# A retention and feed-forward kernel in written order: each engine's sequence fixed by the code, a serial first block, weights converted later, and a new layout of q, k and v

## The chip, the cores and the metric

The kernel runs on one core of one Trainium2 chip. The metric is the device time of one execution in microseconds (us): the median of repeated runs. Times within one execution come from one profiled execution, counted from the start of its span.

## The reference

The kernel computes retention, that is attention with a fixed decay instead of a softmax, and a feed-forward layer on top of it. Batch is 8, heads 8, sequence 576, head size 64; the model width is 512 and the hidden width 2048.

```python
scores = scale * np.matmul(q, k.transpose(0, 1, 3, 2))
gamma = 1.0 - 2.0 ** (-5.0 - np.arange(H, dtype=np.float32))
Dmat = np.where(rel >= 0, gamma[:, None, None] ** rel[None, :, :], 0.0)
attn_out = np.matmul(scores * Dmat[None], v)
x = attn_out.transpose(0, 2, 1, 3).reshape(B * S, H * D)
h = x @ w_in
return (h - np.tanh(h)) @ w_out
```

The two weights are float64 arrays; q, k and v are float32.

## The kernel before

**Chunks.** The sequence is cut into nine chunks of 64 positions. A chunk of all eight batches is a block of 512 columns, and the blocks are numbered n = 0 to 8. Retention runs chunk by chunk with a running state in SBUF: for each batch, scores within the chunk, a mask, the product with v, plus the state times q. q and v are first multiplied by tables of decay powers (`qtab`, `vtab`) on GpSimd (POOL), lines 134 and 135, for the first chunk 328 and 329. Each product is many 64x64 matmuls issued by `run` (L171).

**Items of the feed-forward layer.** The hidden width is 16 tiles f of 128. `mm1(n, f)` is twelve 128x512 matmuls (L229): float32 precision comes from splitting x and the weight into a high and a low part and adding three products. `activate` computes g = h - tanh(h): tanh on ScalarE (ACT, L242), the subtraction on VectorE (DVE, L243), the rounding to the high part `gh` on ACT (L244) and the low part `gl` on DVE (L245). `mm2(n, f)` is twelve matmuls (L278) that add into the PSUM tile `o` of four groups t. At f = 15 the groups are finished one after the other: each group's three matmuls are followed by a copy `ob`, on ACT for t = 0 and 2 (L285), on DVE for t = 1 and 3 (L287), and by two stores.

**Entries.** `entry(p, sc)` is the retention of a pair of batches of the next chunk: 64 small matmuls (scores of pair p+1, outputs and states of pair p), the mask `pm` (L180), the new x in `xh` (ACT, L195) and `xl` (DVE, L196), the state's addition (L216), then the load of pair p+2 and its preparation on POOL. Four entries lie in a chunk.

**The first block.** Chunk 0 has no work to hide behind. Its eight batches j come one at a time, with the data in buffers that w_out takes over later. Scores run two batches ahead of the outputs. Before it, 14 matmuls on a zeroed tile `warm` (L298) keep TensorE (PE) at work. The PSUM tile `spare` holds scores, new state and most of the outputs.

**Weights.** They arrive as float64 and are turned into two float32r parts on the chip: two ACT operations make a guard mask (L62, L63), three DVE operations on integers assemble the bits (L71, L73, L75), ACT rounds the high part (L77) and DVE subtracts the low part (L78). This is called a conversion or a unit; there are 32, 16 for w_in and 16 for w_out. `steps(k)` advances it by a number of DVE operations, `ready(k)` completes k of them.

**The stages.** First the first block; then n = 0 and n = 1, in which only `mm1` runs and h is stored to DRAM (`spill`, copied by ACT at L234) because w_out isn't converted yet; then the 32 spilled items are fetched back (`fetch`), activated (`resume`, L260 to L263) and multiplied (`mm2`); and for n = 2 to 8 a loop of `mm1(n, f)`, an entry where f % 4 == 1, and `mm2` of the item before.

**What sets the order.** A scheduler orders each engine's instructions by estimated times and dependencies; so the order of an engine needn't be that of the code. A dependency is kept per tile: a matmul into one group of `o` waits for a copy that reads another group of it. All loads and stores are issued by SyncE's queue (SP).

## Time and profile before

| | us |
|---|---|
| median of 3 runs | 930.42 (930.21 to 931.33) |
| profiled execution | 931.84 |
| its span | 930.1 |
| PE busy | 895.2 (96%) |
| DVE busy | 367.1 (39%) |
| ACT busy | 282.7 (30%) |
| POOL busy | 97.2 (10%) |
| mean granted TensorE clock | 0.977 |

In the rows of a profile, PE is TensorE's matmuls and PEld its weight loads, which overlap them; L229 is line 229 of the kernel; x12 is a count of instructions. A row of the timeline has the start, the duration, the engine, the line and the operation with out<-in, and in brackets the idle time before it with what released it. A row of the waits has who waited for whom, the total, how often, and the longest. A row of the stages has, after each engine's busy time, the granted clock as a share of full speed, the DMA engines' share and what they moved.

### The profile page before, as it was taken

Reading aid. Unit: us, or ns where it says so; the run is one execution under the profiler, and the core shown is the slowest. Engines: PE = TensorE matmul, PEld = TensorE weight load, DVE = VectorE, ACT = ScalarE, POOL = GpSimd, SP = SyncE. Lnnn points to the kernel's source line nnn. Section 1 sums busy time; section 2 is a strip of 40 time slices with the busy share of each in tenths; the row PEclk is TensorE's granted clock in tenths of the full one; section 3 lists DMA queues with packets and bytes.
Section 4 is the critical chain, followed back from the end, with each engine's and each line's share of the span. In section 5 each row is a group of like instructions: output and inputs, shape, how many; then the busy total and the mean of one; then the engine's idle time right before and its main releaser. Section 6 shows DMA issues by size and latency. Waiting matters only on the chain.

```text
span 930.1 us, 17611 instructions
## 1 busy us (share of the span) xinstructions
PE 895.2 (96%) x7822; PEld 732.7 (79%) x7822; DVE 367.1 (39%) x543; ACT 282.7 (30%) x483; POOL 97.2 (10%) x84
## 2 busy tenths in 40 slices
PE   6698899999999999999999999999999999999997
PEld 4586688787878888888888888888888888888885
DVE  3989911654533333333332343333232332223222
ACT  2686522644422222222222222222222222222221
POOL 5204210000010000000100010001100100000000
PEclk7599899999999999999999999999999999999999
DMA  8787645434231113111311131112111221001001
GB/s 297 283 289 249 265 175 179 116 102 125 81 91 52 47 46 92 52 46 47 92 47 51 45 89 42 39 32 75 53 51 47 66 72 47 1 1 46 1 1 45
DMA packets 27004, 83.11 MB, mean 89 GB/s; under 512 B 3760, under 2 KB 4912, under 8 KB 22832
## 3 DMA queue, kind: packets, MB, share of 16 engines
q1 hardware_dynamic: 26928, 81.99, 27.2%
q8 instruction: 61, 1.00, 0.5%
q14 instruction: 15, 0.12, 0.1%
HBM read 64.15 MB, written 17.83 MB: 88 GB/s over the span
## 4 chain that ended last, share of the span: by engine, by line
PE 88%; DVE 6%; DMA 2%; issue 1%; ACT 1%; POOL 1%; SPq 0%; DVEq 0%; ACTq 0%
PE o L278 43%; PE h L229 38%; PE s L171 3%; PE own L171 2%; PE new L171 2%; DMA a<-in_qkv_dram 1%; DVE mi L71 1%; DVE mi L73 1%; DVE mo L71 1%; DVE wi L78 1%; DMA rwo<-in_w_out_dram 1%; DVE mo L73 1%; DVE mi L75 0%; DMA spill_dram<-g 0%; DVE wo L78 0%
## 5 line engine op out<-in xcount | busy, mean ns | idle before, releaser
L229 PE MATMUL h<-xh,wi 128*128 128x512 f32 x1152 | 309.5, 393 | 1.2 <-ACT xh L195 0.9
L278 PE MATMUL o<-wo,gh 128*128 128x512 f32 x1152 | 294.4, 394 | 4.4 <-ACT gh L262 1.7
L229 PEld LDWEIGHTS h<-xh,wi 128*128 128x128 f32 x1152 | 216.9, 189 | 47.2 <-ACT xh L195 1.1
L278 PEld LDWEIGHTS o<-wo,gh 128*128 128x128 f32 x1152 | 212.4, 188 | 52.9 <-ACT ob L285 3.9
L243 DVE TENSOR_TENSOR g<-h,g 128x512 f32<-128x512 f32 x112 | 77.4, 691 | 375.5 <-ACT g L242 375.5
L242 ACT ACTIVATE g<-h 128x512 f32<-128x512 f32 x112 | 67.0, 598 | 398.7 <-PE h L229 397.8
L278 PE MATMUL o<-wo,gl 128*128 128x512 f32 x576 | 158.5, 389 | 0.0
L229 PE MATMUL h<-xl,wi 128*128 128x512 f32 x576 | 155.1, 391 | 0.0
L229 PEld LDWEIGHTS h<-xl,wi 128*128 128x128 f32 x576 | 108.9, 189 | 23.1
L278 PEld LDWEIGHTS o<-wo,gl 128*128 128x128 f32 x576 | 108.1, 188 | 22.6
L134 POOL TENSOR_TENSOR a<-a,qtab 128x512 f32<-128x512 f32 x32 | 47.6, 1487 | 672.1 <-DMA a<-in_qkv_dram 660.6
L245 DVE TENSOR_TENSOR gl<-g,gh 128x512 fp32r<-128x512 f32 x112 | 84.1, 751 | 74.2 <-ACT gh L244 59.1
L244 ACT CAST gh<-g 128x512 fp32r<-128x512 f32 x112 | 69.5, 620 | 82.3 <-DVE g L243 79.1
L171 PE MATMUL own<-a,state 64*64 64x64 f32 x1024 | 65.4, 224 | 0.0
L171 PE MATMUL own<-pm,a 64*64 64x64 f32 x1024 | 63.7, 222 | 0.0
L171 PEld LDWEIGHTS own<-a,state 64*64 64x64 f32 x1024 | 53.1, 137 | 1.1 <-issue 1.1
L171 PEld LDWEIGHTS own<-pm,a 64*64 64x64 f32 x1024 | 53.1, 138 | 0.4 <-issue 0.4
L171 PEld LDWEIGHTS s<-a 64*64 64x64 f32 x1024 | 33.6, 137 | 22.1 <-issue 12.4
L171 PE MATMUL s<-a 64*64 64x64 f32 x1024 | 38.9, 225 | 8.4 <-POOL a L134 8.4
L135 POOL TENSOR_TENSOR a<-a,vtab 128x512 f32<-128x512 f32 x32 | 38.7, 1211 | 0.0
L216 DVE TENSOR_TENSOR state<-new,state 128x512 f32<-128x512 f32 x28 | 19.2, 686 | 38.8 <-PE own L171 38.8
L171 PE MATMUL new<-a 64*64 64x64 f32 x896 | 33.6, 225 | 0.0
(47 smaller groups left out, 459.3 us busy)
## 6 DMA issues: line engine op xcount, KB each, us to landing
a<-in_qkv_dram SPq DMA_DIRECT2D x32, 1024.0 KB, 5.5
out_dram<-ob SPq DMA_DIRECT2D x72, 128.0 KB, 2.4
rwi<-in_w_in_dram SPq DMA_DIRECT2D x16, 512.0 KB, 10.2
spill_dram<-g SPq DMA_DIRECT2D x32, 256.0 KB, 3.4
rwo<-in_w_out_dram SPq DMA_DIRECT2D x16, 512.0 KB, 5.3
s<-spill_dram SPq DMA_DIRECT2D x32, 256.0 KB, 2.6
a<-in_qkv_dram SPq DMA_DIRECT2D x8, 512.0 KB, 8.8
qtab<-in_qtab_dram SPq DMA_DIRECT2D x9, 128.0 KB, 2.1
```

Source lines behind the costliest of these rows:

```text
L71: nc.vector.scalar_tensor_tensor(z, hw, 3, z, op0=ALU.logical_shift_left, op1=ALU.bitwise_and)
L73: nc.vector.scalar_tensor_tensor(z, lw, 29, z, op0=ALU.logical_shift_right, op1=ALU.bitwise_or)
L134: nc.gpsimd.tensor_tensor(a[:, :, 0], a[:, :, 0], qtabs[c].unsqueeze(1).broadcast_to([P, 2, 4, C]), op=ALU.mult)
L135: nc.gpsimd.tensor_tensor(a[:, :, 2], a[:, :, 2], vtab[:, c].unsqueeze(1).unsqueeze(3).broadcast_to([P, 2, 4, D]), op=ALU.mult)
L171: nc.tensor.matmul(out_, w, x, start=start, stop=stop)
L216: nc.vector.tensor_tensor(st, new, st, op=ALU.add)
L229: nc.tensor.matmul(hp, win[f][:, a, cc, :], x[:, cc, :], start=(k == 0), stop=(k == 3 * NCC - 1))
L242: nc.scalar.activation(g, h, AF.Tanh)
L243: nc.vector.tensor_tensor(g, h, g, op=ALU.subtract)
L244: nc.scalar.copy(gh, g)
L245: nc.vector.tensor_tensor(gl, g, gh.bitcast(F32), op=ALU.subtract)
L278: nc.tensor.matmul(o[:, t], g[:, t * P : (t + 1) * P], wout[f][:, a, :], start=(f == 0 and k == 0), stop=(f == NF - 1 and k == 2),)
```

## The change

The change has five parts. A new function adds, at the end of the program, a dependency from each instruction to the one before it on its engine, so that every engine issues in the order in which the code is written. The first block is one batch at a time, with filler matmuls on `warm` after the scores and after the outputs, a PSUM tile of its own for the new state, and an early Tanh on ACT on which the warm-up's matmuls wait. The conversion is cut into units of three steps, with the low part's subtraction put into the next unit's first step; a step stands before and two behind each `mm1` of n = 0 and of three in four f of n = 1, and the rest goes with the resumed items. q, k and v are laid out in DRAM with each batch of a chunk contiguous (a pair's load then has two pieces of 4 KB for each partition instead of one of 8 KB). The first table `qtab0` gets a place in a buffer that w_out's eighth tile takes later, so that `qtab1` needn't wait for its last use.

```diff
+def in_order(tc):
+    before = {}
+    for ins in tc.nc.cur_bb.bb.instructions:
+        if ins.engine in before:
+            tc.add_manual_dep(
+                ins, before[ins.engine],
+                mybir.DependencyInfo(mybir.DependencyClass.NoSync, mybir.DependencyReason.DATA), reason="in_order",
+            )
+        before[ins.engine] = ins.name
...
+    def unit(k):
+        t, f = stream[k]
+        hw, lw = wraw[t, f][:, :, 1], wraw[t, f][:, :, 0]
+        z = masks.pop((t, f))
         nc.vector.scalar_tensor_tensor(z, hw, 3, z, op0=ALU.logical_shift_left, op1=ALU.bitwise_and)
+        finish()
         yield
+        if 0 < k and k + 1 < at_["load"]:
+            upto("guard", k + 2)
         nc.vector.scalar_tensor_tensor(z, lw, 29, z, op0=ALU.logical_shift_right, op1=ALU.bitwise_or)
         yield
         nc.vector.scalar_tensor_tensor(z, hw, -0x40000000, z, op0=ALU.bitwise_and, op1=ALU.bitwise_or)
...
         nc.scalar.copy(w[:, 0], z.bitcast(F32))
-        nc.vector.tensor_tensor(w[:, 1], z.bitcast(F32), w[:, 0].bitcast(F32), op=ALU.subtract)
...
+        last.append((w, z))
+    def finish():
+        while last:
+            w, z = last.pop()
+            nc.vector.tensor_tensor(w[:, 1], z.bitcast(F32), w[:, 0].bitcast(F32), op=ALU.subtract)
...
-            qtabs[c] = pool.tile([P, 4, C], F32, tag="qtab", bufs=1, name=f"qtab{c}")
+            if c == 0:
+                qtabs[c] = const.tile([P, 4, C], F32, tag="wo7", name="qtab0")
...
-        nc.sync.dma_start(a, qkv_d[c, :, 2 * pr : 2 * pr + 2])
+        nc.sync.dma_start(a, qkv_d[c, 2 * pr : 2 * pr + 2].rearrange("u p t i s -> p u t i s"))
...
     nc.vector.memset(warm, 0.0)
+    nc.scalar.activation(warm[:, :1], warm[:, :1], AF.Tanh)
...
+        sc, o = spare[:, j % 2, :4], spare[:, 2 + j % 2, :4]
+        new = psp.tile([P, 4, D], F32, tag="h", bufs=2, name=f"new_first{j}")
+        run(m_score(j, sc), [])
+        busy(1, 64)
+        after_score(j, sc.unsqueeze(1), 1)
+        if 4 <= j < 7:
+            step()
         run(m_state(j, new), m_out(j, o))
+        if j < B - 1:
+            busy(1, 64)
+        else:
+            busy(4)
         after_out(j, o.unsqueeze(1), 1)
         nc.scalar.copy(state[:, j], new)
...
+    units(2)
+    prep(B // 2)
     prep(B // 2 + 1)
...
-            upto("load", 9 + 3 * f // 4 if n == 0 else NF + 4 + f)
-            ready(f + 3 if n == 0 else NF + 3 * (f + 1) // 4)
+            upto("load", 10 + 3 * f // 4 if n == 0 else NF + 5 + f)
+            if n == 0 or f % 4 < 3:
+                step()
             mm1(n, f)
+            if n == 0 or f % 4 < 3:
+                step()
+                step()
...
-        if n == 0:
-            ready(NF + 12 + (f + 2) // 2)
+        for _ in range(2):
+            step()
         mm2(n, f)
...
     mm2(*prev)
+    in_order(tc)
```

The first place is PE in the first block, at batch 0. Before, with `a_86` and `a_90` the data of batches 0 and 1, and `pm_140` the masked scores of batch 0:

```order
L171 MATMUL spare<-a_86 64x64 [waits DMAHW1_49,Pool_49]
L171 MATMUL spare<-a_86 64x64 x7
L171 MATMUL spare<-a_90 64x64 [waits DMAHW4_49,DVE_49,Pool_49]
L171 MATMUL spare<-a_90 64x64 x7
L171 MATMUL spare<-a_86 64x64 [waits DVE_49]
```

And now, with `a_87` and `a_91` the same two batches, `pm_142` batch 0's masked scores and `new_first` its new state:

```order
L189 MATMUL spare<-a_87 64x64 [waits DMAHW1_49,Pool_49]
L189 MATMUL spare<-a_87 64x64 x7
L318 LDWEIGHTS warm
L318 MATMUL wps<-warm 64x512
L189 MATMUL new_first_132<-a_87 64x64 [waits Pool_49]
L189 MATMUL new_first_132<-a_87 64x64
L189 MATMUL spare<-pm_142,a_87 64x64 [waits DVE_49]
```

Batch 1's scores stood ahead of batch 0's state and outputs; now they stand behind them and a second filler, and wait for DVE there.

The second place is ACT at the end of chunk 2, where `g_0` and `gh_0` belong to item (3, 0), `ob_0` and `ob_2` to chunk 2's output. Before:

```order
L244 CAST gh_15_3362<-g_15_3361 128x512
L242 ACTIVATE g_0_3393<-h_0_3380 128x512
L285 COPY ob_0_3403<-o_2689 128x512
L244 CAST gh_0_3394<-g_0_3393 128x512
L285 COPY ob_2_3417<-o_2689 128x512
```

And now:

```order
L262 CAST gh_15_3389<-g_15_3388 128x512
L260 ACTIVATE g_0_3420<-h_0_3407 128x512
L262 CAST gh_0_3421<-g_0_3420 128x512
L303 COPY ob_0_3430<-o_2716 128x512
L303 COPY ob_2_3444<-o_2716 128x512
```

The first copy has moved behind item (3, 0)'s cast.

The third place is PE at the same chunk end, where `h_1` is item (3, 1) and `o` chunk 2's output. Before, from the first group on:

```order
L278 MATMUL o_2689<-wo_2006,gl_15_3363 128x512 [waits DVE_49]
L229 MATMUL h_1_3428<-xh_2680,wi_399 128x512 x4
L278 MATMUL o_2689<-wo_2006,gh_15_3362 128x512 [waits Activation_49]
L278 MATMUL o_2689<-wo_2006,gh_15_3362 128x512
L278 MATMUL o_2689<-wo_2006,gl_15_3363 128x512
L229 MATMUL h_1_3428<-xl_2681,wi_399 128x512 x4
```

And now:

```order
L296 MATMUL o_2716<-wo_1952,gl_15_3390 128x512 [waits DVE_49]
L296 MATMUL o_2716<-wo_1952,gh_15_3389 128x512 [waits Activation_49]
L296 MATMUL o_2716<-wo_1952,gh_15_3389 128x512
L296 MATMUL o_2716<-wo_1952,gl_15_3390 128x512
L296 MATMUL o_2716<-wo_1952,gh_15_3389 128x512 [waits DVE_49]
L296 MATMUL o_2716<-wo_1952,gh_15_3389 128x512
```

The matmuls of item (3, 1) stood between the groups; now they stand behind the last group. In the same way the matmuls of items (2, 0) and (2, 1), which stood between the last `mm1` of n = 1 and the first resumed `mm2`, now stand behind all 32 resumed items.

More of the change, by code (lines that the diff above doesn't have):

```diff
@@ L64, in guard @@
         masks[t, f] = m
-    def convert(t, f):
-        raw = wraw.pop((t, f))
-        hw, lw = raw[:, :, 1], raw[:, :, 0]
+    def unit(k):
+        t, f = stream[k]
+        hw, lw = wraw[t, f][:, :, 1], wraw[t, f][:, :, 0]
         z = masks.pop((t, f))
-        w = const.tile([P, 2, DM], F32R, tag=f"w{t}{f}", name=f"w{t}{f}")
         nc.vector.scalar_tensor_tensor(z, hw, 3, z, op0=ALU.logical_shift_left, op1=ALU.bitwise_and)
+        finish()
         yield
+        if 0 < k and k + 1 < at_["load"]:
+            upto("guard", k + 2)
         nc.vector.scalar_tensor_tensor(z, lw, 29, z, op0=ALU.logical_shift_right, op1=ALU.bitwise_or)
@@ L75, in convert @@
         nc.vector.scalar_tensor_tensor(z, hw, -0x40000000, z, op0=ALU.bitwise_and, op1=ALU.bitwise_or)
-        yield
+        del wraw[t, f]
+        w = const.tile([P, 2, DM], F32R, tag=f"w{t}{f}", name=f"w{t}{f}")
         nc.scalar.copy(w[:, 0], z.bitcast(F32))
-        nc.vector.tensor_tensor(w[:, 1], z.bitcast(F32), w[:, 0].bitcast(F32), op=ALU.subtract)
-        if t == "o":
-            wout[f] = w
-        else:
-            win[f] = w.rearrange("p s (c m) -> p s c m", m=P)
+        (wout if t == "o" else win)[f] = w if t == "o" else w.rearrange("p s (c m) -> p s c m", m=P)
+        last.append((w, z))
[3 more added lines that the diff above has]
+            nc.vector.tensor_tensor(w[:, 1], z.bitcast(F32), w[:, 0].bitcast(F32), op=ALU.subtract)
     stream = [(t, f) for t in "io" for f in range(NF)]
     at_ = {"load": 0, "guard": 0, "convert": 0}
-    going = []
+    last, going = [], []
     def upto(what, n):
@@ L91, in upto, with step, units @@
             at_[what] += 1
-    def steps(n):
-        for _ in range(n):
-            if not going:
-                if at_["convert"] == 2 * NF:
-                    return
-                upto("guard", at_["convert"] + 1)
-                going.append(convert(*stream[at_["convert"]]))
-                at_["convert"] += 1
-            if next(going[0], "end") == "end":
-                going.pop()
-    def ready(n):
+    def step():
+        if not going:
+            if at_["convert"] == 2 * NF:
+                return finish()
+            upto("guard", at_["convert"] + 1)
+            going.append(unit(at_["convert"]))
+            at_["convert"] += 1
+        if next(going[0], "end") == "end":
+            going.pop()
+    def units(n):
         while at_["convert"] < min(n, 2 * NF) or going:
-            if at_["convert"] < n:
-                upto("guard", at_["convert"] + 2)
-            steps(1)
+            step()
     loaded, scored, xs, qtabs = {}, {}, {}, {}
@@ L115, in load_qtab @@
         if c not in qtabs:
-            qtabs[c] = pool.tile([P, 4, C], F32, tag="qtab", bufs=1, name=f"qtab{c}")
+            if c == 0:
+                qtabs[c] = const.tile([P, 4, C], F32, tag="wo7", name="qtab0")
+            else:
+                qtabs[c] = pool.tile([P, 4, C], F32, tag="qtab", bufs=1, name=f"qtab{c}")
             nc.sync.dma_start(qtabs[c], qtab_d[c])
@@ L293, in retention_ffn, with busy @@
     nc.vector.memset(warm, 0.0)
+    nc.scalar.activation(warm[:, :1], warm[:, :1], AF.Tanh)
     wps = psp.tile([P, BLK], F32, tag="new", bufs=1, name="wps")
-    def busy(n):
+    def busy(n, rows=P):
         for _ in range(n):
-            nc.tensor.matmul(wps, warm[:, :P], warm, start=True, stop=True)
+            nc.tensor.matmul(wps[:rows], warm[:rows, :rows], warm[:rows], start=True, stop=True)
     busy(WARM)
-    load_qtab(0)
     def load_first(j):
         loaded[j] = const.tile([P, 4, 4, C], F32, tag=f"wo{NF - 1 - j}", name=f"a{j}")
-        nc.sync.dma_start(loaded[j], qkv_d[0, :, j])
+        nc.sync.dma_start(loaded[j], qkv_d[0, j])
+    load_qtab(0)
     load_first(0)
@@ L315, in retention_ffn @@
         load_first(j)
-    upto("load", 4)
+    upto("load", 5)
     load_pair(B // 2)
-    upto("load", 6)
+    upto("load", 7)
     load_pair(B // 2 + 1)
-    upto("load", 8)
+    upto("load", 9)
     spare = psp.tile([P, 4, 8, C], F32, tag="o", bufs=1, name="spare")
-    owns = [spare[:, 3, :4], spare[:, 3, 4:], psp.tile([P, 4, C], F32, tag="own", bufs=1, name="own_first")]
-    def first_prep(j):
+    for j in range(B):
         a = loaded[j]
@@ L329, in first_prep @@
         nc.gpsimd.tensor_tensor(a[:, 2], a[:, 2], vtab[:, 0].unsqueeze(2).broadcast_to([P, 4, D]), op=ALU.mult)
-    def first_score(j):
-        run(m_score(j, spare[:, j % 3, :4]), [])
-        after_score(j, spare[:, j % 3, :4].unsqueeze(1), 1)
-    first_prep(0)
-    first_prep(1)
-    first_score(0)
-    first_score(1)
-    for j in range(B):
-        if j + 2 < B:
-            first_prep(j + 2)
-        if j == B - 2:
-            prep(B // 2)
-        new, o = spare[:, j % 3, 4:], owns[j % 3]
+        sc, o = spare[:, j % 2, :4], spare[:, 2 + j % 2, :4]
[5 more added lines that the diff above has]
+            step()
         run(m_state(j, new), m_out(j, o))
+        if j < B - 1:
+            busy(1, 64)
+        else:
+            busy(4)
         after_out(j, o.unsqueeze(1), 1)
         nc.scalar.copy(state[:, j], new)
-        if j + 2 < B:
-            first_score(j + 2)
-        if 3 <= j < 7:
-            steps(1)
+    units(2)
+    prep(B // 2)
     prep(B // 2 + 1)
@@ L380, in retention_ffn @@
             resume(*late[k + 1])
-        if n == 0:
-            ready(NF + 12 + (f + 2) // 2)
+        for _ in range(2):
+            step()
         mm2(n, f)
@@ L419, in _layouts @@
     q, k, v = heads(q), heads(k), heads(v)
-    cols = np.stack([q, k]).transpose(4, 2, 6, 1, 0, 3, 5).reshape(NC, P, B, 2, 4, C)
-    rows = np.stack([v, k]).transpose(4, 2, 5, 1, 0, 3, 6).reshape(NC, P, B, 2, 4, D)
+    cols = np.stack([q, k]).transpose(4, 1, 2, 6, 0, 3, 5).reshape(NC, B, P, 2, 4, C)
+    rows = np.stack([v, k]).transpose(4, 1, 2, 5, 0, 3, 6).reshape(NC, B, P, 2, 4, D)
     w = w_in.reshape(2, 4, D, NF, P)[::-1]
```

## The prediction

> **What bounds the kernel now.** I read the page first, then the busy time by stage, then the waits, and last the timeline at the places that the change touches.

> ```profile
> PE 895.2 (96%) x7822; PEld 732.7 (79%) x7822; DVE 367.1 (39%) x543; ACT 282.7 (30%) x483; POOL 97.2 (10%) x84
> ...
> 20.00:40.00 20.00, 11.32 (x244) 10.02 (x244) 17.67 (x29) 11.41 (x25) 6.72 (x6) 0.59 0.91 351
> 80.00:100.00 20.00, 16.91 (x191) 13.28 (x189) 19.93 (x31) 13.57 (x25) 5.80 (x2) 1.00 0.72 263
> 112.00:164.00 52.00, 52.00 (x703) 43.13 (x702) 10.32 (x15) 12.28 (x21) 9.81 (x8) 1.00 0.48 169
> 266.00:931.00 665.00, 657.17 (x5440) 540.43 (x5438) 206.47 (x299) 155.18 (x257) 53.10 (x44) 1.00 0.16 48
> ```

> The columns of a stage are its length, busy time of PE, PEld, DVE, ACT and POOL, the granted clock, the DMA share and GB/s. From 266 on PE is the bound: 657 of 665 us. Only before 112 is there much to win: at 20 to 40 PE works 11.3 of 20 us at a clock of 0.59, and at 80 to 100 it is VectorE that is full (19.93 of 20). So the change can save some twenty microseconds at the front, and anything it puts into the stage after 266 is paid in full, seven chunks long.

> PE's unit is twelve matmuls of 128x512:

> ```profile
> 272.29 2.72 PE h L229 x12
> ...
> 311.93 2.95 PE o L278 x12
> ...
> 335.94 2.95 PE o L278 x12
> ...
> 360.43 2.95 PE o L278 x12
> ```

> An item is 2.72 us, 0.227 a matmul. From 311.93 to 335.94 lie 24.01 us: eight items and one entry, which is thus 24.01 - 21.76 = 2.25. From 335.94 to 360.43 lie 24.49: the end of chunk 2 lies in it, and costs 0.48.

> **The first block.** Before:

> ```profile
> 1.19 5.59 PE L298 MATMUL wps<-warm 128*128 128x512 bf16 x14 [1.19 <-DVE warm L293]
> 6.71 0.68 PE L171 MATMUL spare<-a 64*64 64x64 f32 x16
> 7.44 0.42 DVE L180 TENSOR_TENSOR pm<-spare,mask 128x256 f32<-128x256 f32 x1 [6.31 <-PE spare L171]
> 9.81 1.12 PE L171 MATMUL spare<-a 64*64 64x64 f32 x16 [2.42 <-POOL a L328]
> 11.48 1.28 ACT L195 ACT_TABLE_LOAD   x1 [11.48 <-DVE pm L180]
> 12.78 0.37 ACT L195 CAST xh<-spare 128x256 fp32r<-128x256 f32 x1
> 13.18 0.42 DVE L196 TENSOR_TENSOR xl<-spare,xh 128x256 fp32r<-128x256 f32 x1 [1.78 <-ACT xh L195]
> 19.72 0.72 POOL L328 TENSOR_TENSOR a<-a,qtab 128x256 f32<-128x256 f32 x1
> 42.15 2.50 PE L229 MATMUL h<-xh,wi 128*128 128x512 f32 x5 [0.88 <-ACT xh L195]
> ```

> The last item's data are ready at 19.72, but the first mm1 starts at 42.15: the items' short operations stand in DVE's and ACT's queues among the conversion's. After, an item has only its own chain: score 0.68, pm 0.42, out and state about as long as the score, xh 0.37, xl 0.42, and some 0.06 of semaphore after each of five steps (7.44 against 6.71 + 0.68): 2.87. The order shows that the next item's scores wait for this xl, so the eight chains stand in a row, and that the warm-up now waits for ACT's table load. That moves the warm-up from 1.19 to about 2.7 (memset, 1.28, latency), its end to 8.3. First mm1: 8.3 + 8 x 2.87 = 31.3, with the last fillers lying beside xh and xl. Gain 42.15 - 31.3 = **10.9**. Bounds: 24 if only data and POOL pace it (19.72 plus an item), 37 if the clock stays low (score 1.12, so 3.7 an item: 8.3 + 29). I take the warm chain, since filler and items together keep PE at 1.84 of 2.87 us.

> **The first two chunks' mm1.** Before, from 42.15 to the last copy of n=1:

> ```profile
> 88.67 1.52 DVE L78 TENSOR_TENSOR wo<-mo,wo 128x512 fp32r<-128x512 f32 x1
> 90.11 0.68 DVE L71 SCALAR_TENSOR_TENSOR mo<-rwo,mo 128x512 int32<-128x512 int32 x1
> 90.72 0.68 DVE L78 TENSOR_TENSOR wo<-mo,wo 128x512 fp32r<-128x512 f32 x1
> ...
> PEld s L171 <- POOL a L134: 9.7, 3, 4.5
> ...
> 97.78 1.07 PE L229 MATMUL h<-xh,wi 128*128 128x512 f32 x4
> 102.94 0.37 PE L171 MATMUL s<-a 64*64 64x64 f32 x2 [4.09 <-POOL a L134]
> ...
> 163.13 0.59 ACT L234 COPY g<-h 128x512 f32<-128x512 f32 x1 [2.13 <-PE h L229]
> ```

> That is 121.0 us for 32 x 2.72 + 8 x 2.25 + 1.1 = 106.1 of work, 14.9 lost: three waits for POOL's preparation (9.7 on the weight loads), the last with a fall of the clock behind it, and the conversion that filled VectorE. A conversion takes four DVE operations at a pitch of 0.61 (90.72 after 90.11), 2.4 us, under an item's 2.72; so one unit an item, as written now, just fits, and twelve go to n=1, where DVE had 10 of 52 us to do. What stays: a first wait of about 1.4 for the second unit, and while POOL prepares, DVE's 0.68 becomes 1.52 and its own preparation is longer too. I put 3.5 on n=0 for that and 0.5 on n=1: 5.4 lost, 111.5, gain **9.5**. Bounds: 108 (only the unit's wait and 0.5) to 121 (nothing gained). The two 4 KB pieces for one of 8 KB and qtab0's own place I cost at nothing of their own: in n=1, 52.00 of 52.00 busy, no entry waited for its pair, and in n=0 a landing that is shorter or longer moves only the waits for POOL, inside the bounds just given.

> **From n=1 into the resumed items.**

> ```profile
> 169.50 2.14 PE L278 MATMUL o<-wo,gh 128*128 128x512 f32 x8 [1.69 <-ACT gh L262]
> ...
> 265.99 2.00 PE L278 MATMUL o<-wo,gh 128*128 128x512 f32 x8
> 268.89 0.68 PE h L229 x3
> ```

> Copy, spill, fetch, tanh, subtraction and cast take 163.13 to 169.50, 6.37. The chain stays as long, but PE filled all but 1.69 of it with chunk 2's matmuls; in written order it idles, and loses another 2.2 to the low clock after (an estimate; the price of a fall is below). Then before: 169.50 to 265.99, 96.5, until chunk 2's first mm2, with only three matmuls of h(2,2) left to do. After: 32 items 87.0; the two block ends without filler 4.1 and 3.0 over an item, by the rows below; 0.5 for late units on DVE; mm1(2,0), mm1(2,1) and the entry 7.7; nine matmuls of h(2,2) 2.0: 104.3. Together **+10.0** (2 to 12).

> **Six chunk ends in the steady stage.** Here the order is worth more than the front. The program's last item has the written order's structure, with no matmuls to fill in:

> ```profile
> 916.72 1.98 PE L278 MATMUL o<-wo,gh 128*128 128x512 f32 x8
> 916.92 0.60 ACT L242 ACTIVATE g<-h 128x512 f32<-128x512 f32 x1 [3.47 <-PE h L229]
> 918.27 0.62 ACT L244 CAST gh<-g 128x512 fp32r<-128x512 f32 x1 [0.76 <-DVE g L243]
> 920.32 0.59 ACT L285 COPY ob<-o 128x512 f32<-128x512 f32 x1 [1.42 <-PE o L278]
> 920.95 0.73 PE L278 MATMUL o<-wo,gh 128*128 128x512 f32 x2 [0.68 <-ACT ob L285]
> 922.76 0.73 PE L278 MATMUL o<-wo,gh 128*128 128x512 f32 x2 [0.84 <-DVE ob L287]
> 924.40 0.73 PE L278 MATMUL o<-wo,gh 128*128 128x512 f32 x2 [0.68 <-ACT ob L285]
> ```

> Each of o's four groups waits for the copy of the one before. Now ob0 also stands behind gh(n+1,0) on ACT. From the end of h(n+1,0): gh ends 2.17 later (918.27 + 0.62 - 916.72), ob0 starts at 2.07 (ACT's pitch), group 1 at 2.70 (920.95 - 920.32 later), group 2 at 4.51, group 3 at 6.15 and the next item at 6.95, where 2.72 would do. So 4.23 a chunk end, less today's 0.48: 3.75, six times **+22.5**. Lower bound 1.5 less each if ob0 did not wait for gh; no reason gives less.

> The clock comes on top:

> ```profile
> 6.10:9.50 3.40, 1.29 (x19) 0.64 (x17) 0.42 (x1) 0.00 (x0) 1.08 (x3) 1.00 0.94 317
> 9.51:12.91 3.40, 2.25 (x48) 1.88 (x48) 0.42 (x1) 1.42 (x2) 3.38 (x6) 0.50 1.03 410
> 33.40:36.80 3.40, 1.54 (x36) 1.13 (x33) 3.40 (x6) 1.46 (x3) 1.63 (x2) 1.00 1.03 413
> 36.84:40.24 3.40, 1.24 (x36) 1.05 (x40) 3.37 (x7) 2.49 (x6) 0.00 (x0) 0.50 0.72 282
> 100.00:112.00 12.00, 9.06 (x148) 7.97 (x149) 11.93 (x17) 6.76 (x13) 3.36 (x3) 0.72 0.69 257
> ```

> The two stretches at 6.10 and 33.40, 38% and 45% busy, are each followed by one at a clock of 0.50 (the last column but two), though PE was never idle for the whole of one. At a chunk end, 3.41 us can hold as little as 0.8 of PE's work (23%) or 47%, by where they fall. A stretch of 3.4 at half clock costs 1.7, two 3.4; 100 to 112, with the fall at the 4.09 wait, lost 0.28 x 12 = 3.4 of clock, some of it in the wait. I take 2.4 a fall, and a fall at three ends of six: **+7.2** (0 to 15). [...]

> **Sum.** -10.9 - 9.5 + 10.0 + 22.5 + 7.2 = +19.3. The profiled execution took 931.84 (span 930.1), 1.42 over the median; on the median 930.42 + 19.3 = **949.7**. A difference of 0.2%, 1.9 us, is about what a measurement of this kernel can tell from none.

> **Rivals.**
> - *PE runs past the waiting groups (faster).* If h(n+1,1)'s ready matmuls ran while group 1 waits, the six ends would cost nothing new and no clock would fall: 949.7 - 22.5 - 7.2 = 920. It decides from the first chunk end on. Against it: at 97.78 to 102.94 PE stood 4.09 us before one waiting entry, though the mm1 behind it had its operands. [...] 5%.
> - *No clock falls at the ends*: 949.7 - 7.2 = 942.5. For it: the ends' work is large matmuls, the two stretches were small ones. 13%.
> - *Clock falls at all six*: 949.7 + 7.2 = 956.9. For it: 47% is near the 45% that fell. 17%.
> - *The front gains little*: cold items, first mm1 at 37 (+5.7), and n=0 and n=1 as bound by loads and POOL as now (+9.5): 964.9. For it: the clock of 0.59 at 20 to 40, with a DMA share of 0.91. 8%.
> - *The front gains more*: the items run at the pace of the data, first mm1 at 24: 942.4. Against it, the written wait of scores for xl. 11%.

> That the change doesn't do what it says is out: its order is as described above.

> **Chances and range.** The forecast has 46%. The range 935 to 962 takes in both cases at 942 together (935) and all six falls with part of a poor front; left out are the first rival and the end of the poor front. Faster by over 0.2%: the first rival and 2% for a front at its lower bounds with cheap ends, 7%. Within 0.2%: 3%. Slower: 90%.

> **What would show it.** Right: first mm1 near 31; the last copy of n=1 near 143; no matmul between it and the first resumed mm2; at each chunk end PE rows of o with waits for ob, ob0 behind gh, 6.9 us per last item; clock falls at some of these. Wrong: mm1 rows among o's groups at a chunk end, ob0 ahead of gh, or a first mm1 past 37.

## The result and the profile after

The changed kernel takes 970.45 us (median of four runs, 969.42 to 971.9) against 930.41 before: a ratio of 1.043, with a 95% interval of 1.041 to 1.045. It is slower, as forecast, but by 40.0 us where 19.3 were forecast, and outside the range of 935 to 962. The profiled execution took 970.24, its span is 968.5.

The counts of instructions have hardly changed, PE is busy 20 us longer, and the clock's row shows something new:

```profile
PE 915.3 (95%) x7840; PEld 738.5 (76%) x7841; DVE 366.1 (38%) x543; ACT 283.5 (29%) x484; POOL 88.6 (9%) x84
...
PEclk9799998989999989999999989997999899998999
```

Behind the first eighth, the row of before had only nines. In this one the two eights in slices 7 and 9 are the handover to the resumed items and the end of the first resumed block, and the eights and sevens from slice 15 on are chunk ends, some 103 us apart. (The end at 454 lies across two slices, and both still show a nine.) The stages show the same in numbers:

```profile
34.07:147.00 112.93, 109.22 (x1442) 87.45 (x1440) 101.14 (x141) 73.67 (x127) 20.01 (x15) 1.00 0.72 253
147.00:153.02 6.02, 0.00 (x1) 0.00 (x1) 0.71 (x2) 1.89 (x4) 2.23 (x2) 0.79 0.59 177
153.02:254.12 101.10, 94.38 (x385) 74.88 (x386) 48.73 (x75) 40.81 (x70) 0.00 (x0) 0.94 0.32 92
262.50:968.50 706.00, 678.79 (x5471) 552.74 (x5460) 203.88 (x302) 156.03 (x259) 51.35 (x44) 0.97 0.15 45
```

The columns are as in the prediction, the granted clock the last but two. The first row is n = 0 and n = 1: PE now works 109 of 113 us. The second is the handover to the resumed items: PE does nothing. In the last, the steady stage, PE is idle for 27 of 706 us where it was for 8 of 665, and the clock is 0.97 instead of 1.00.

The first block, with the starts of the scores of batches 2 and 3 (batches are counted from 0), then 5 and 6, and the first mm1:

```profile
13.52 0.68 PE L189 MATMUL spare<-a 64*64 64x64 f32 x16 [0.87 <-issue]
16.38 0.68 PE L189 MATMUL spare<-a 64*64 64x64 f32 x16 [0.87 <-POOL a L345]
...
22.60 1.12 PE L189 MATMUL spare<-a 64*64 64x64 f32 x16 [0.74 <-issue]
26.33 1.12 PE L189 MATMUL spare<-a 64*64 64x64 f32 x16 [0.76 <-issue]
...
34.07 1.46 PE L247 MATMUL h<-xh,wi 128*128 128x512 f32 x4
```

An item takes 2.86 at first (forecast 2.87) and 3.73 after the clock has fallen (the prediction's cold item has 3.7). The stretch before the fall and the one behind it:

```profile
17.39:20.80 3.41, 2.06 (x60) 1.66 (x63) 1.21 (x4) 1.84 (x4) 0.61 (x2) 1.00 1.02 407
20.81:24.21 3.40, 2.66 (x50) 2.03 (x46) 1.24 (x4) 0.65 (x2) 0.00 (x0) 0.50 1.04 406
```

One chunk end, that of chunk 2:

```profile
351.23 0.61 PE L296 MATMUL o<-wo,gh 128*128 128x512 f32 x2
...
352.79 0.62 ACT L262 CAST gh<-g 128x512 fp32r<-128x512 f32 x1 [0.76 <-DVE g L261]
353.31 0.58 ACT L303 COPY ob<-o 128x512 f32<-128x512 f32 x1
...
353.94 0.73 PE L296 MATMUL o<-wo,gh 128*128 128x512 f32 x2 [1.87 <-ACT ob L303]
...
355.75 1.22 PE L296 MATMUL o<-wo,gh 128*128 128x512 f32 x2 [0.84 <-DVE ob L305]
...
358.07 1.23 PE L296 MATMUL o<-wo,gh 128*128 128x512 f32 x2 [0.67 <-ACT ob L303]
```

The copy stands behind the next item's cast, and the three waits are there: 1.87, 0.84, 0.67. From group 0 to group 1 it is 2.71, where 2.70 was forecast. The first two matmuls of groups 2 and 3 then take 1.22 instead of 0.73: the clock has fallen in the middle of the end, from 1.00 to 0.50 at 355.3. All six ends have these three waits (1.87, 0.84, and 0.67 or 0.68), and in each of them the clock fell to 0.50.

### The profile page after: what moved, and what is told of

The parts are those of the page before. It is cut to its first block, busy times and chain, and to the rows that moved or that the text cites. A ratio compares the mean times of both kernels' runs of the same rounds, so it can differ in the third digit from the quotient of the medians.

```text
span 968.5 us, 17623 instructions
## 1 busy us (share of the span) xinstructions
PE 915.3 (95%) x7840; PEld 738.5 (76%) x7841; DVE 366.1 (38%) x543; ACT 283.5 (29%) x484; POOL 88.6 (9%) x84
## 5 line engine op out<-in xcount | busy, mean ns | idle before, releaser
L296 PE MATMUL o<-wo,gh 128*128 128x512 f32 x1152 | 305.7, 405 | 35.2 <-ACT ob L303 19.3
L247 PE MATMUL h<-xh,wi 128*128 128x512 f32 x1152 | 313.9, 398 | 3.7 <-ACT wi L93 2.2
L296 PEld LDWEIGHTS o<-wo,gh 128*128 128x128 f32 x1152 | 216.8, 192 | 94.6 <-ACT ob L303 28.9
L247 PEld LDWEIGHTS h<-xh,wi 128*128 128x128 f32 x1152 | 219.8, 192 | 53.7 <-ACT wi L93 3.7
L296 PE MATMUL o<-wo,gl 128*128 128x512 f32 x576 | 162.8, 397 | 0.0
L296 PEld LDWEIGHTS o<-wo,gl 128*128 128x128 f32 x576 | 110.7, 192 | 23.6
L152 POOL TENSOR_TENSOR a<-a,qtab 128x512 f32<-128x512 f32 x32 | 42.5, 1328 | 713.5 <-DMA a<-in_qkv_dram 704.7
L263 DVE TENSOR_TENSOR gl<-g,gh 128x512 fp32r<-128x512 f32 x112 | 78.6, 702 | 76.8 <-ACT gh L262 74.7
L262 ACT CAST gh<-g 128x512 fp32r<-128x512 f32 x112 | 69.4, 620 | 84.9 <-DVE g L261 84.9
L281 DVE TENSOR_TENSOR gl<-s,gh 128x512 fp32r<-128x512 f32 x32 | 22.2, 692 | 36.1 <-PE o L296 26.5
L280 ACT CAST gh<-s 128x512 fp32r<-128x512 f32 x32 | 19.9, 621 | 40.7 <-PE o L296 27.7
## 6 DMA issues: line engine op xcount, KB each, us to landing
rwi<-in_w_in_dram SPq DMA_DIRECT2D x16, 512.0 KB, 10.9
```

What stands on the lines that cost most here:

```text
L152: nc.gpsimd.tensor_tensor(a[:, :, 0], a[:, :, 0], qtabs[c].unsqueeze(1).broadcast_to([P, 2, 4, C]), op=ALU.mult)
L247: nc.tensor.matmul(hp, win[f][:, a, cc, :], x[:, cc, :], start=(k == 0), stop=(k == 3 * NCC - 1))
L262: nc.scalar.copy(gh, g)
L263: nc.vector.tensor_tensor(gl, g, gh.bitcast(F32), op=ALU.subtract)
L280: nc.scalar.copy(gh, g)
L281: nc.vector.tensor_tensor(gl, g, gh.bitcast(F32), op=ALU.subtract)
```

## Experiments

**Fillers at the chunk ends.** What is the waits' share, and what the clock's? Matmuls of no use were put into the waits of the six steady chunk ends; the output is not touched by them.

```diff
+                if 2 <= n < NC - 1 and t < 3:
+                    if t == 0:
+                        wps2 = psp.tile([P, BLK], F32, tag="new", bufs=1, name=f"wps{n}")
+                    for _ in range((8, 3, 3)[t]):
+                        nc.tensor.matmul(wps2, wout[0][:, 0, :P], wout[1][:, 0], start=True, stop=True)
```

> The changed kernel with matmuls of no use in the three waits at each of the six chunk ends of the steady stage: 8 behind group 0, 3 behind group 1, 3 behind group 2, on converted weights, into the PSUM tile of new states, which is free there; their results are not read. The waits for the copies stay as long as they were. Theory, that the ends' cost is the waits (about 3.8 each) and on top a fall of the clock (about 2.8 each): the clock stays at 1.00 there and the period of a chunk goes from 103.1 to about 100.3, in all 6 x 2.8 = 17 less, 953. Rival, that what goes beyond the waits is something else than the clock (stores, a late item behind the end): the period stays within 1 us of 103.1, or grows by the fillers, and the time is 965 or more.

Measured: 954.09 (953.55 to 956.15), ratio 1.025 to before (1.024 to 1.027). The same chunk end, and the stage:

```profile
351.14 0.62 PE L296 MATMUL o<-wo,gh 128*128 128x512 f32 x2
...
351.82 1.98 PE L310 MATMUL wps<-wo,wo 128*128 128x512 f32 x8
...
353.86 0.73 PE L296 MATMUL o<-wo,gh 128*128 128x512 f32 x2
...
358.11 1.07 PE L247 MATMUL h<-xh,wi 128*128 128x512 f32 x4
```

```profile
262.00:951.00 689.00, 681.81 (x5583) 557.96 (x5572) 203.97 (x303) 156.27 (x259) 50.36 (x44) 1.00 0.15 46
```

From group 0 to the next item lie 6.97 us, where 6.95 was forecast: the copies are waited for exactly as long, with the filler in the place of idle time. The clock stays at 1.00. So the 970.45 - 954.09 = 16.4 us are the clock's, 2.7 a chunk end on average over the six.

**The output tile cut in four.** The waits exist only because a dependency is kept per tile. With a tile for each group, in the first block too, and everything else as in the changed kernel, the written order included:

```diff
-            ops[n] = psp.tile([P, 4, DM], F32, tag="o", bufs=1, name=f"o{n}")
+            ops[n] = [psp.tile([P, DM], F32, tag=f"o{t}", bufs=1, name=f"o{n}_{t}") for t in range(4)]
...
-    spare = psp.tile([P, 4, 8, C], F32, tag="o", bufs=1, name="spare")
+    spare = [psp.tile([P, 8, C], F32, tag=f"o{t}", bufs=1, name=f"spare{t}") for t in range(4)]
...
-        sc = psp.tile([P, 4, 2, 4, C], F32, tag="o", bufs=1, name=f"s{n}_{f}")
-        return sc[:, 0]
+        return psp.tile([P, 2, 4, C], F32, tag="o0", bufs=1, name=f"s{n}_{f}")
```

> The changed kernel, order and all, with the output tile cut into four tiles of one PSUM bank each, and the first block's tile likewise, so that a group waits for no copy of another group. Theory, that waits per tile in written order make the loss: the six chunk ends cost under 0.5 each (-37), the two ends of the resumed items nothing over an item with no fall of the clock (-10), and in the first block the next scores no longer wait for xl (some 0.8 an item, -6): about 917. Rival, that copies on ACT behind the cast, or stores, hold PE as before: 955 or more. A second rival, that the first block is paced by its data: ends as said, first mm1 still at 32 or later, about 923.

Measured: 915.25 (914.03 to 915.91), ratio 0.983 (0.981 to 0.984): faster than both kernels. The first mm1, and the steady stage:

```profile
26.66 1.28 PE L247 MATMUL h<-xh,wi 128*128 128x512 f32 x4
```

```profile
254.00:914.00 660.00, 653.47 (x5437) 540.87 (x5436) 201.91 (x298) 154.29 (x257) 50.38 (x44) 1.00 0.16 48
```

PE is idle for 6.5 of the 660 us, and the clock is 1.00: the steady ends cost nothing any more. The first mm1 came 7.4 earlier, so neither the data nor POOL held it to 34.07, but the waits per tile, the scores' wait for xl above all, with the low clock that came with them (it fell for one stretch of 3.41 us here, from 19.30 to 22.71, and for four in the changed kernel). Not all of this reaches the end: the last copy of n = 1 starts at 143.13, 3.9 earlier than 147.00. In the two profiled executions 3.9 of the gain lie before that copy, 7.7 between it and chunk 2's first mm2, and 42.8 behind.

**Without the written order.** The changed kernel, its last line taken away:

```diff
     mm2(*prev)
-    in_order(tc)
```

> The changed kernel without the added dependencies, so that the scheduler orders each engine as it did in the kernel before. Theory, that the written order alone makes the loss, and the other parts of the change are as good as forecast: chunk ends and resumed items as in the kernel before, the front up to 20 shorter, 910 to 925. Rival, that the gain of the front comes from the written order too: the scheduler puts the conversion among the first block's items again, first mm1 past 38, 925 to 935. Second rival, that the late conversion or the layout costs more than it brings: over 935.

Measured: 928.21 (926.86 to 931.62), ratio 0.997 (0.996 to 0.998): the first rival's numbers. The first mm1:

```profile
39.36 1.22 PE L247 MATMUL h<-xh,wi 128*128 128x512 f32 x2 [0.47 <-ACT xh L213]
```

The scheduler avoids the chunk ends' loss, and gives back two thirds of the first block's gain: 39.4 instead of 34.1 in written order, and 42.2 before. The change without the written order is thus worth 2.8 us (against 930.98, the kernel before in the same session).

**The written order alone**, put on the kernel before:

```diff
+def in_order(tc):
...
     mm2(*prev)
+    in_order(tc)
```

> The kernel before with the added dependencies alone: written order, nothing else changed. Theory: its chunk ends lose the same 6.6 less 0.5 each, six times 37, its resumed items' ends 10, the handover without chunk 2's matmuls 8; its front keeps its loss or is worse, since the code has two conversions ready ahead of each mm1: 975 to 1000. Rival, that the written order costs only with the changed front: under 950.

Measured: 996.31 (994.18 to 999.86), ratio 1.070 (1.068 to 1.073), in the forecast interval, at its far end. So the written order by itself costs 65 us on the old code, and the change's other parts, with it, win 26 of them back. Its trace has the same three waits at the chunk ends, and a handover of 8.9:

```profile
174.14 3.51 PE L290 MATMUL o<-wo,gh 128*128 128x512 f32 x8 [8.88 <-ACT gh L274]
```

**The copy ahead of the next activation.** The changed kernel, with a chunk's first activation written behind the last mm2 of the chunk before:

```diff
+        elif n > 2 and f == 0:
+            return lambda: activate(n, f, hp, g)
...
-            mm1(n, f)
+            later = mm1(n, f)
...
                 mm2(*prev)
+            if later:
+                later()
```

> The changed kernel with the activation of a chunk's first item written behind the last mm2 of the chunk before, so that on ACT the copies ob0 and ob2 stand ahead of that item's tanh and cast; the matmuls stand as in the changed kernel. Theory: the first wait at the six chunk ends goes from 1.87 to 0.68, as in the program's last item, 1.2 an end; and since the resumed items' ends with the same three waits (0.67, 0.85, 0.68) fell in clock too, the falls stay: 970 - 7 = 963. Rival, that the longest wait is what makes the clock fall: without it four or more of the six ends keep the clock, 7 + 4 x 2.8 or more less: 952 or below.

Measured: 950.18 (945.61 to 952.03), ratio 1.022 (1.019 to 1.024). The theory's 963 fell; the rival held. The first wait is 0.68 as expected, which is worth 7 us; the other 13 go with falls of the clock that did not take place. In the profiled execution, the shortest of the four, five of six ends kept the clock. An end that kept it, by two stretches, and the one that lost it, with the stretch behind it; then a resumed end, which this edit does not touch, with the stretch behind it:

```profile
744.12:747.52 3.40, 2.58 (x11) 1.48 (x9) 0.05 (x1) 0.58 (x1) 0.00 (x0) 1.00 0.00 1
747.53:750.93 3.40, 2.04 (x8) 1.38 (x9) 0.65 (x2) 1.08 (x2) 0.00 (x0) 1.00 0.66 152
846.52:849.91 3.39, 1.91 (x7) 1.29 (x8) 0.69 (x1) 1.08 (x2) 0.00 (x0) 0.99 0.68 160
849.93:853.32 3.39, 3.39 (x10) 2.62 (x9) 1.98 (x3) 0.62 (x1) 0.00 (x0) 0.51 0.68 160
...
201.31:204.70 3.39, 1.88 (x6) 0.91 (x6) 0.69 (x1) 1.08 (x2) 0.00 (x0) 1.00 0.67 155
204.72:208.11 3.39, 3.39 (x15) 2.79 (x16) 1.38 (x2) 0.74 (x2) 0.00 (x0) 1.00 0.67 166
```

The stretches are 3.41 us long, cut where the clock changes. The same three waits fall differently into them from end to end: 60% busy at the least in the first pair, 56% in the third row, and there the clock fell. But the resumed end's stretch, 55% busy, kept the clock, and so did the other resumed end (1.00 from 240 to 260); in the changed kernel both lost it (0.50 from 201.7 and from 252.9), with the same waits. So in these rows PE's share of one stretch does not tell a fall (56%) from none (55%). The spread of this kernel's four times, 6.4 us with granted clocks of 0.974 to 0.985, fits with falls that come in some executions and not in others; how many ends fell in the other three is not shown.

**Chunk 2's first matmuls ahead of the resumed items.** On the kernel with the cut tiles:

```diff
     fetch(0, 0)
     fetch(0, 1)
+    early = [mm1(2, f, True) for f in range(2)]
...
+        if k == len(late) - 1:
+            early[0]()
         mm2(n, f)
+    early[1]()
...
-            mm1(n, f)
+            if n > 2 or f > 1:
+                mm1(n, f)
```

> The kernel with the output tile cut in four, in written order, and with the 24 matmuls of chunk 2's first two items written ahead of the resumed items (their activations behind the last but one of these). Theory, that the handover costs its idle 5.9 and a fall of the clock: both go, 5.4 of matmuls and some 2.2 of clock, 907 to 908. Rival, that the resumed items are paced by their fetch and activation: the wait is found again between the first resumed items, 911 to 915.

Measured: 909.55 (908.79 to 910.04), ratio 0.977 (0.975 to 0.979). Of the 7.6 forecast 5.7 came, which lies between the theory and its rival:

```profile
145.88 1.07 PE L247 MATMUL h<-xh,wi 128*128 128x512 f32 x4
147.38 1.89 PE L298 MATMUL o<-wo,gh 128*128 128x512 f32 x7 [0.43 <-ACT gh L282]
```

The handover's 6 us are filled but for 0.43, and the clock doesn't fall: it is 1.00 from 140 to 215. Waits of 1.0 and 1.65 before the third and fifth resumed item remain, as the rival had it.

**No fillers in the first block.** The changed kernel without the single fillers behind scores and outputs:

```diff
         run(m_score(j, sc), [])
-        busy(1, 64)
...
-        if j < B - 1:
-            busy(1, 64)
-        else:
+        if j == B - 1:
             busy(4)
```

> The changed kernel without the one filler matmul behind each score and behind each output of the first block (the last four fillers stay). In the changed kernel the clock fell at 20.8 in spite of them and the first mm1 came at 34.1. Theory, that the fillers delay the fall: without them it falls by 14, four items more at 3.7 instead of 2.86, first mm1 near 37, in all 972 to 974. Rival, that the fillers bring nothing or lie in the way: first mm1 at 34.1 or before, 968 to 971.

Measured: 971.12 (968.78 to 971.41), ratio 1.043 (1.041 to 1.045): not to be told from the changed kernel. The first mm1 came at 35.35, not 37. Without the fillers the clock fell to 0.50 at 12.3, 8.5 us sooner, and an item then took the same 3.73; but the first score started at 6.97 instead of 7.79, as the warm-up took 4.76 instead of 5.58. The theory held for the clock; that the fillers win anything in the whole time is not shown.

**The old layout and the old place of the first table**, each on the kernel with the cut tiles:

```diff
-        nc.sync.dma_start(a, qkv_d[c, 2 * pr : 2 * pr + 2].rearrange("u p t i s -> p u t i s"))
+        nc.sync.dma_start(a, qkv_d[c, :, 2 * pr : 2 * pr + 2])
...
-        nc.sync.dma_start(loaded[j], qkv_d[0, j])
+        nc.sync.dma_start(loaded[j], qkv_d[0, :, j])
...
```

> The kernel with the output tile cut in four, with q, k and v laid out as in the kernel before (a pair's load in one piece of 8 KB a partition, a batch's of 4 KB with a stride). Theory, that the layout costs and brings nothing: 915.3 within 1.8. Rival, that a contiguous batch lands sooner and with it the first block's data, which were ready 3 us earlier in the changed kernel than before: first mm1 2 to 3 us later, 917 to 919.

Measured: 915.55 (914.52 to 916.07).

And the other:

```diff
-            if c == 0:
-                qtabs[c] = const.tile([P, 4, C], F32, tag="wo7", name="qtab0")
-            else:
-                qtabs[c] = pool.tile([P, 4, C], F32, tag="qtab", bufs=1, name=f"qtab{c}")
+            qtabs[c] = pool.tile([P, 4, C], F32, tag="qtab", bufs=1, name=f"qtab{c}")
```

> The changed kernel with the cut tiles, with the first table back in the pool, so that the load of the second table waits for the last use of the first and holds up SyncE's queue behind it. Theory, that the other loads of the front keep the DMA engines occupied until then: 915 to 917. Rival, that the loads behind it come late for the first mm1s, as in the kernel before: 919 or more.

Measured: 914.98 (914.06 to 915.12). Against 915.25 neither part of the change makes a difference in the kernel with the cut tiles. They were costed at nothing, which holds there.

**The cut tiles without the written order**, on the old code and on the new. On the old code, beside the output tile's cut as above:

```diff
-    spare = psp.tile([P, 4, 8, C], F32, tag="o", bufs=1, name="spare")
-    owns = [spare[:, 3, :4], spare[:, 3, 4:], psp.tile([P, 4, C], F32, tag="own", bufs=1, name="own_first")]
+    spare = [psp.tile([P, 8, C], F32, tag=f"o{t}", bufs=1, name=f"spare{t}") for t in range(4)]
+    owns = [spare[3][:, :4], spare[3][:, 4:], psp.tile([P, 4, C], F32, tag="own", bufs=1, name="own_first")]
...
```

> The kernel before, ordered by its scheduler, with the output tile and the first block's tile cut into four tiles of one bank. Theory, that the scheduler hid the waits between groups at 0.5 a chunk end and 1.5 to 2 at a resumed end: some 6 less, 923 to 927. Rival, that the cut alone is worth what it was worth in the changed kernel, also in the first block: 915 or below. Second rival, that the scheduler makes another order of it and loses the gain: 930 or more.

Measured: 911.14 (909.95 to 913.62), ratio 0.978 (0.976 to 0.981). The theory fell and the rival held: the cut alone, in the kernel before, is worth 20 us.

```profile
24.75 1.65 PE L229 MATMUL h<-xh,wi 128*128 128x512 f32 x3 [0.91 <-ACT xh L195]
```

Its first mm1 comes at 24.75 instead of 42.15. Seven of the conversion's DVE operations stand before it, where 27 did: with the tiles cut, the scheduler also makes another order, so this run by itself does not tell the waits per tile from the conversion's place.

On the new code, the kernel with the cut tiles without its last line:

```diff
     mm2(*prev)
-    in_order(tc)
```

> The changed kernel with the cut tiles, but without the added dependencies. It tells what the written order is worth once no group waits for another. Theory, that the written order then brings the front's gain and costs only the handover: without it first mm1 near 38 again and the resumed items' handover filled, 919 to 925. Rival, that the order no longer matters: within 2 of 915.3.

Measured: 914.70 (914.15 to 915.39), against 915.25 in written order: the rival held. Once no group waits for another, the order makes no difference to the time on the new code. And the old code with the cut tiles, 911.14, is some 3.5 us shorter than the new code with them in the same session (four runs each, without overlap): with the tiles cut, the change wins nothing more, in either order.

## Why the prediction was wrong

The terms, measured between the two profiled executions (span +38.4; 1.6 more on the medians):

| term | forecast | measured |
|---|---|---|
| first mm1 | -10.9 | 34.07 - 42.15 = -8.1 |
| n = 0 and n = 1 | -9.5 | (147.00 - 34.07) - 121.0 = -8.1 |
| handover and resumed items | +10.0 | +14.9 |
| six chunk ends, waits and clock | +29.7 | +39.6 |

For the third, PE's first mm2 of chunk 2 starts at 262.74, so 115.7 us after 147.00 against 102.9 before, and the nine matmuls of h(2,2) come on top; for the last, 705.8 us remain against 664.1, less the same nine.

- **The waits were right.** 22.5 us for the six chunk ends: the fillers' kernel shows 6.97 from group 0 to the next item, the prediction 6.95.
- **The clock's term failed.** The step was "a fall at three ends of six", 2.4 each, 7.2 in all. All six fell, at 2.7 to 2.9 each: 16.4 by the fillers' kernel, 17.1 by the table less the 22.5, above the 0 to 15 that the term was given. The prediction had the evidence in hand: stretches at an end that can be as little as 23% busy or 47%, and two falls at 38% and 45%; the stretches before the six falls were 34 to 45% busy. For three of six it gives no row; it lies midway between two cases, where the rows spoke for one of them. The rival "clock falls at all six" got 17%. With this term at its measured 17.1 the sum would be 959.6, inside the range; the falls that no term held took the time out of it.
- **It failed in the other terms too.** The two resumed ends have the same short waits and the clock fell there as well, which no term held; in 153.02 to 254.12 the clock was 0.94, 6.1 us lost where 2.2 were put down. In the run with the copy ahead of the activation (950.18), where both kept the clock, the stretch from n = 1's last copy to chunk 2's first mm2 is 3.2 shorter (147.40 to 259.95). So of the 4.9 that this term missed, some 3 to 4 are the clock's; a wait of 1.48 between resumed items is most of the rest. And the first block's clock fell at 20.8 in spite of the fillers, after a stretch 60% busy (the prediction had an item with its fillers at 1.84 of 2.87, and took that for enough): its last four items took 3.4 more than four warm ones, and as the first score started 0.5 before the forecast, its gain fell short by 2.8. Together the clock accounts for some 16 of the 19 us that were missed between the profiled executions (an estimate from these sums).
- **A cause was misread.** The prediction put the late first mm1 of the kernel before down to the conversion's instructions among the items'. The old code in written order has only four of the conversion's DVE operations ahead of the first mm1, not 27, and still starts it at 38.44; with the cut tiles and the scheduler's order it starts at 24.75 behind seven of them. That speaks for the waits per tile on the first block's tile as the larger part, though no run took away the one alone. The sum was not hurt by it, since the new chain was worked out with that wait in it.
- **Layout and table**: costed at nothing, and nothing on the kernel with the cut tiles.
- **A small slip**: eight items of 3.7 behind 8.3 end at 37.9, not 37; only the bound and the rival of a poor front rest on it.

At all eight ends of the changed kernel, six in the steady stage and two in the resumed items, the clock fell to 0.50, with no idle time of PE over 1.87 us. In none of the eight did a matmul of the next item start ahead of a waiting group.

## What to carry to other kernels

Before fixing an engine's order by hand, look for the waits that the present order hides: here a PSUM tile with four groups made each group wait for the copy of another (1.87, 0.84 and 0.67 us at a chunk end in written order), and the scheduler, which filled the waits, concealed them (the chunk ends cost 0.48 each before). Cutting the tiles was worth 20 us here on the old code in the scheduler's order and 55 on the new code in written order; without the cut, the change's other parts won 2.8 in the scheduler's order and 26 in the written one. And price a chain of short waits on TensorE as the waits plus the clock: here the waits of a chunk end made it 4.25 us longer than an item (6.97 less 2.72), and the fall of the clock cost another 2.7.

## What the runs showed of the hardware

```profile
454.31:457.70 3.39, 1.52 (x6) 0.68 (x5) 1.39 (x2) 1.70 (x3) 0.00 (x0) 1.00 0.00 0
198.31:201.70 3.39, 1.86 (x8) 0.97 (x6) 1.13 (x2) 0.58 (x1) 0.00 (x0) 1.00 0.33 76
...
959.48:962.87 3.39, 1.88 (x7) 0.92 (x7) 0.69 (x1) 0.58 (x1) 0.00 (x0) 1.00 0.50 114
```

The first, 45% busy, and the second, 55%, were each followed by a clock of 0.50; the third, 55% too, was not. In the first block, a stretch of small matmuls 60% busy (17.39 to 20.80) was followed by a fall. No one share of busy time parts these rows, and no run shows what does.

In the changed kernel the clock went back to 1.00 behind stretches 90% busy or more; stretches of 78% and 80% at 0.50 were followed by another at 0.50. In the kernel without the first block's fillers the clock went back behind one of 83%:

```profile
770.09:773.48 3.39, 2.82 (x7) 2.25 (x8) 0.69 (x1) 0.51 (x1) 0.00 (x0) 0.50 0.52 117
773.50:776.90 3.40, 3.40 (x84) 2.72 (x84) 0.54 (x1) 0.60 (x1) 0.00 (x0) 1.00 0.34 81
```

A fall at one of the six chunk ends lasted two stretches, 6.83 us (at the first from 355.3 to 362.1), at one of them three, 10.24, and cost 2.7 us on average (16.4 for the six), where the longest wait is 1.87.
